# Parameter tables in a new order, late tiles and first spectral operands in steps, and the last chunk's weights loaded together: a long convolution beside a feed-forward network on one core of Trainium2

## The chip, the core and the metric

The kernel runs on one core of a Trainium2 chip. The metric is the device time of one execution in microseconds, as the median of several runs. The kernel before was run three times: 1127.53, 1129.48 and 1130.53 us, so its median is 1129.48 us. One further execution was recorded by the hardware profiler.

## The reference, cut to what matters

The input `u` has 2048 positions of 576 features. It is normalized over its features, and two branches start from the result: a state-space layer, whose convolution kernel is built from complex parameter tables of 576 x 128, and a feed-forward network. Input and both branches are added.

```python
xn = layernorm(u)                                # u: 1 x 2048 x 576
dt = exp(log_dt)[:, None]
A, Bc, Cc = A_re + 1j*A_im, B_re + 1j*B_im, C_re + 1j*C_im       # 576 x 128
P  = exp((dt*A)[:, :, None] * arange(2048))
K  = einsum("dn,dnl,dn->dl", Cc, P, dt*Bc).real  # 576 x 2048
y  = causal_convolution(xn, K) + xn * Dskip      # by FFT of length 4096
ff = silu(xn @ w1) @ w2                          # 576 -> 4608 -> 576
out = u + y + ff
```

All is in float32.

## The kernel before, in words

**Precision.** A product of two float32 matrices is made of three matmuls: each operand is split into a high part (a cast by ScalarE, ACT in the profile) and a low part (a subtraction by VectorE, DVE), and high x high, high x low and low x high are added up in PSUM. So each operand that comes from memory needs one ACT and one DVE instruction ahead of its first matmul.

**The feed-forward network is the frame.** `ffn` runs over two halves of 1024 positions, in each over nine chunks of 512 hidden features (`NCH` = 9), and in each chunk over two blocks of 512 positions. A chunk has four tiles of weights (`FT` = 4). `up(blk, t)` makes one tile of hidden values: 14 matmuls of 128x512 into `ph` (L291 to L293), then SiLU (L299), the high part `gh` (L300, ACT) and the low part `gl` (L301, DVE). `down(blk, jj)` takes 128 positions back to 576 features: 2 x 12 matmuls of 128x288 into `po` (L316), each dozen of which DVE adds to `acc` (L320). `ph` has two buffers in PSUM, `po` three. The weights of the next chunk are loaded and split between these steps: `load_w1` (L247 to L249, two tiles at once, one buffer `w1r`), `split_w1` (L260 on ACT, L262 on DVE), `load_w2` (L269, two buffers `w2r`) and `split_w2` (L278, L280). A table `after` (around L371) says after which step which of these stands; the same table held for all chunks.

**The other work is woven in.** `weave` runs through the 288 steps of the network and lets a generator, `side` (from L786), issue its next piece when a fraction of the steps has gone by; the fractions are written by hand. `side` issues in this order:

- `phase0` for the first eight tiles of 128 positions, in pairs: load (L164), layernorm (`normed`, with statistics at L180 and the normalization at L189), transposes, and stores of the normalized tile (`dxn`, L231) and of its transposes (`dxt`, L230).
- `natural` (L396 to L517), which makes the tables of the convolution kernel from the parameters, in four steps: loads (L407, L420), powers by ACT's functions, a root with its corrections (L450 to L459, the store `dexp` at L460), products, three reciprocals (L475), a second part and the store `dmag` (L517). Between them stands `phase0` for the eight later tiles, in four pairs (8, 10, 12, 14), each with load and normalization in one step, at 0.02, 0.035, 0.06 and 0.08. Their input buffer `xj` has one copy.
- `kgen` (L519 to L663), which generates the kernel and stores it as `d1k` (L659, L662), from 0.13 to 0.595 (`marks`), and between its pieces `spread`, which writes the transformed input `d1u` to memory.
- `spectral` (L665 to L706), 32 steps from 0.595 to 0.822: `front(k)` loads a tile of `d1u` and of `d1k` and splits it (`load_split`, L743 to L746, with `split_of`, L737 to L741), multiplies by the transform's matrices (`mm3`, L754, into `pu`, `pk` and `pb`) and stores the result `d`.
- `tail` (from L710): the last stage of the convolution, woven into the last chunk. `conv_load` (L761) loads `ys` from `d`, four tiles ahead, L716 loads the first half's results `r`, `add_conv` (L774 on TensorE, L780 on DVE) adds them, and L171 stores the output.

**Who sets the order.** The order in which a program issues its pieces fixes priorities; a scheduler then sorts the instructions of each engine by them, and `behind(...)` keeps an instruction from being sorted ahead of a named one. Each engine runs its own list strictly in order. Nearly all loads and many stores are issued by SyncE (SP), whose list is one queue: an issue that waits for a free buffer holds up all behind it.

Of the kernel before, what the change touches and what calls it, by code (L numbers as in the profile page):

```python
# [2 lines left out]

# [7 lines left out]
F32 = mybir.dt.float32  # L11
# [6 lines left out]
P = 128  # L18
# [23 lines left out]
def kernel(  # L42
# [91 lines left out]
    def behind(ins):  # L134
        return tc.issue_after(ins) if ins is not None else nullcontext()
# [61 lines left out]

    def phase0(p0, js):
        j0 = js[0]
        if j0 < 8:  # L200
            xs = load_x(j0, accp, "acc", (nc.sync, nc.scalar) if j0 < 4 else (nc.sync,))
            acc.update(zip(js, xs))
        else:
            xs = load_x(j0, p0, "xj", (nc.sync,))
        if j0:
            normed(p0, js, xs)
        else:
            for j, xj in zip(js, xs):
                normed(p0, (j,), (xj,))
# [23 lines left out]
    def ffn():  # L233
# [6 lines left out]
        def load_w1(half, c, t):  # L240

            f = c * FT + t
            first = half == 0 and c == 0
            r1 = (pa if first and t else wp).tile([P, 5, 2 * P], F32, tag="w1r", name="w1r", bufs=1)
            fs = slice(f * P, (f + 2) * P)
            eng = nc.gpsimd if first and t == 0 else nc.sync
            eng.dma_start(r1[:, 0:4, :], w1[0:512, fs].rearrange("(k p) f -> p k f", p=P))  # L247
            eng.dma_start(r1[0:64, 4, :], w1[512:576, fs])
            pins["load"] = eng.dma_start(r1[64:128, 4, :], w1[512:576, fs]).ins  # L249
            R1[half, c, t] = r1  # L250
# [14 lines left out]
        def load_w2(half, c, t):  # L265

            first = half == 0 and c == 0
            r2 = (pa if first and t > 1 else wp).tile([P, D], F32, tag="w2r", name="w2r", bufs=2)
            pins["load"] = nc.sync.dma_start(r2, w2v[:, c * FT + t, :]).ins  # L269
            R2[half, c, t] = r2  # L270

# [91 lines left out]
        for i, blk in enumerate(blocks):  # L363
            half, c, b = blk
            later = i + 1 < len(blocks)
            new = (half, c + 1) if c + 1 < NCH else (half + 1, 0)
            more = new[0] < 2
            if half == 0 and c == NCH - 1:
                next_xt(b)

            after = {  # L371
                (0, "u0"): [(load_w1, 0)],
                (0, "u1"): [(split_w1, 0), (load_w2, 0), (load_w2, 1)],
                (0, "u2"): [(load_w1, 2)],
                (1, "u0"): [(split_w1, 2), (split_w2, 0), (load_w2, 2)],
                (1, "d3"): [(split_w2, 1), (load_w2, 3), (split_w2, 2)],
                (1, "u2"): [(split_w2, 3)],
            }
            for step in ("u0", "d0", "d1", "d2", "d3", "u1", "u2", "u3"):
                k = int(step[1])  # L380
                if step[0] == "d":
                    down(blk, k)
                    yield 3.0
                elif later:
                    up(blocks[i + 1], k)
                    yield 3.0
                for f, t in after.get((b, step), ()) if more else ():
                    f(*new, t)
                if half == 0 and c == NCH - 1:
                    for kt in {"d3": (0, 1), "u1": (2, 3), "u2": (4,)}.get(step, ()):  # L390
                        split_xt(b, kt)
# [4 lines left out]
    def natural(nat):  # L396
# [55 lines left out]
        nc.scalar.activation(r, r, AF.Square)  # L452
        for i in range(0, 4 * D, D):

            c = slice(i, i + D)
            e = nat.tile([P, D], F32, tag="lrT", name="e")
            v.scalar_tensor_tensor(e, ex[:, c], 1.0, r[:, c], op0=ALU.subtract, op1=ALU.mult)
            v.scalar_tensor_tensor(r[:, c], e, 2.0, r[:, c], op0=ALU.add, op1=ALU.mult)
            v.scalar_tensor_tensor(ex[:, c], ex[:, c], 1.0, r[:, c], op0=ALU.add, op1=ALU.mult)  # L459
# [18 lines left out]

        v.tensor_mul(t1, t0, t0)
        v.tensor_scalar(t1, t1, 1.0, None, op0=ALU.add)  # L480
        yield

        with behind(pins["gh"]):
# [179 lines left out]
                            dskip.unsqueeze(0).broadcast_to([32, D]), accum_op=ALU.add)  # L663

    def spectral():  # L665
        def front(k):
            if k % 2 == 0:
                mm = kl.tile([P, 2, 4, P], F32R, tag="mm", name="mm")
                nc.gpsimd.dma_start(mm, cm23[:, k:k + 2])
                mats.append(mm)  # L670
            mk = mats[-1][:, k % 2]
            us, ks = load_split(d1u[k * P:(k + 1) * P, :], "u"), load_split(d1k[k * P:(k + 1) * P, :], "k")
            ka = kl.tile([P, D], F32, tag="ka", name="ka")
            kb = kl.tile([P, D], F32, tag="kb", name="kb", bufs=1)
            y = kl.tile([P, D], F32, tag="y", name="y", bufs=1)
# [65 lines left out]
        nc.vector.tensor_sub(l, t, h)  # L741
        return h, l

    def load_split(rows, tag):
        t = kl.tile([P, D], F32, tag=tag + "r", name=tag + "r")
        nc.sync.dma_start(t, rows)  # L746
        return split_of(t, tag)

    def mm3(dst, terms, hs):

# [34 lines left out]

    def side():  # L786
        nonlocal s4, kl, yp, pa, tail_at
        marks = (0.13, 0.595, 0.822)
        tail_at = (0.895, 0.0045, 0.922, 0.005)
        with tc.tile_pool(name="pa", bufs=4) as pa:  # L790
            for js in ((0, 1), (2, 3), (4, 5), (6, 7)):
# [6 lines left out]
        with tc.tile_pool(name="kf", bufs=1) as kfp:  # L798
            for n in ("f", "phi"):
                kf[n] = kfp.tile([P, D], F32, name=n + "T")  # L800
            with tc.tile_pool(name="nat", bufs=1) as nat, tc.tile_pool(name="pb", bufs=1) as pb:
                nt = natural(nat)
                tiles = iter(range(8, NJ, 2))
                for at, tables in ((0.0, 1), (0.02, 0), (0.035, 0), (gate_of(1), 1), (0.06, 0), (gate_of(2), 1), (0.08, 0), (0.085, 1)):
                    yield at
                    if tables:
                        next(nt, None)
                    else:
                        j = next(tiles)
                        with behind(pins["gl"]):  # L810
                            phase0(pb, (j, j + 1))
            with behind(pins["sd"]):
                nc.gpsimd.dma_start(f1, cf1)
            nc.sync.dma_start(vt, cv)
            with tc.tile_pool(name="up", bufs=1) as up:
                sp = spread(up)
                for n, at in enumerate(kgen()):
                    if n > 1:
                        next(sp, None)
                    yield marks[0] + at * (marks[1] - marks[0])  # L820
                for _ in sp:
                    pass
# [98 lines left out]
```

## Time and profile before

| what | value |
|---|---|
| median of the runs | 1129.48 us (1127.53 to 1130.53) |
| profiled execution | 1131.96 us |
| its span | 1130.2 us |
| mean granted clock of TensorE | 0.996 |
| chain that ended last | PE 86%, DVE 5%, DMA 5% |
| HBM read, written | 102.53 MB, 44.61 MB |

The profile shows each engine's busy time, its waits by line with what ended them, windows with the busy time, clock and DMA share, a timeline, and the chain of work that ended last, which is followed back from the last instruction. PE is TensorE's matmuls, PEld its loading of weights, SP the engine that issues DMAs. A row such as `PE po L316 <- DVE acc L320` reads: TensorE, about to write `po` in line 316, sat idle until VectorE's line 320 on `acc` was done. In slices of 28 us, the engine TensorE is at nine tenths or more but for the first ones, one in between and the last:

```profile
PE   6999899999999999999999999999999999999998
DVE  6698899999999999999999936887778778774433
DMA  9346531334242625254743345554445455336971
```

### The profile page before, as it was taken

How to read it: one execution, taken by the hardware profiler on the slowest of the kernel's cores; microseconds unless marked ns; L12 is line 12 of the kernel's file. 1: busy time of each engine (PE TensorE's matmuls, PEld its weight loads, DVE VectorE, ACT ScalarE, POOL GpSimd, SP SyncE). 2: the span in 40 equal slices, each digit the busy share in tenths (PEclk: the TensorE clock that was granted, in tenths of full speed). 3: DMA queues.
4: the chain of work that ended last, by engine and by line, in shares of the span. 5: the costliest groups of instructions: out<-in, count | busy, mean ns of one | idle time of the engine just before them, and what ended most of it. 6: DMA issues, size and time to landing. Idle time of an engine off the chain costs nothing.

```text
span 1130.2 us, 22881 instructions
## 1 busy us (share of the span) xinstructions
PE 1106.7 (98%) x9144; PEld 998.7 (88%) x9144; DVE 917.1 (81%) x1545; ACT 708.7 (63%) x1229; POOL 78.5 (7%) x130
## 2 busy tenths in 40 slices
PE   6999899999999999999999999999999999999998
PEld 5988799898888989999889998999999999998776
DVE  6698899999999999999999936887778778774433
ACT  4665356767677676676766727787777787772211
POOL 1110100000000000010000000000000000000110
PEclk9999899999999999999999999999999999999999
DMA  9346531334242625254743345554445455336971
GB/s 272 116 121 173 150 86 57 82 107 106 93 105 70 145 65 116 83 124 153 205 152 88 88 86 170 168 164 130 144 142 168 128 169 149 110 104 168 251 189 56
DMA packets 174971, 148.56 MB, mean 131 GB/s; under 512 B 110944, under 2 KB 141680, under 8 KB 174736
## 3 DMA queue, kind: packets, MB, share of 16 engines
q1 hardware_dynamic: 164768, 112.07, 37.6%
q0 software_dynamic: 9712, 34.14, 9.4%
q8 instruction: 72, 1.18, 0.4%
q10 hardware_dynamic: 384, 0.89, 0.3%
q14 instruction: 35, 0.29, 0.1%
HBM read 102.53 MB, written 44.61 MB: 130 GB/s over the span
## 4 chain that ended last, share of the span: by engine, by line
PE 86%; DVE 5%; DMA 5%; SPq 1%; issue 1%; ACT 0%; POOL 0%; DVEq 0%; POOLq 0%; ACTq 0%
PE po L316 36%; PE ph L291 30%; PE kp L631 3%; PE ph L292 3%; PE ph L293 2%; PE pk L754 2%; PE pu L754 2%; PE pb L754 2%; DMA w1r<-in_B_w_dram 2%; PE z L646 2%; PE pu L153 1%; DMA xj<-in_A_u_dram 1%; PE py L774 1%; PE pu L154 1%; DMA d1k<-stage 1%
## 5 line engine op out<-in xcount | busy, mean ns | idle before, releaser
L316 PE MATMUL po<-w2h,gh 128*128 128x288 f32 x1152 | 338.8, 297 | 6.4 <-DVE acc L320 5.7
L316 PE MATMUL po<-w2h,gl 128*128 128x288 f32 x1152 | 338.5, 297 | 1.0 <-DVE gl L301 1.0
L316 PE MATMUL po<-w2l,gh 128*128 128x288 f32 x1152 | 339.4, 296 | 0.0
L316 PEld LDWEIGHTS po<-w2h,gh 128*128 128x128 f32 x1152 | 216.1, 188 | 16.5 <-DVE acc L320 7.0
L316 PEld LDWEIGHTS po<-w2l,gh 128*128 128x128 f32 x1152 | 216.8, 188 | 4.3
L316 PEld LDWEIGHTS po<-w2h,gl 128*128 128x128 f32 x1152 | 216.5, 189 | 3.5 <-DVE gl L301 1.5
L299 ACT ACTIVATE gf<-ph 128x512 f32<-128x512 f32 (+1 forms) x148 | 86.5, 584 | 140.1 <-PE ph L293 124.7
L320 DVE TENSOR_TENSOR acc<-po,acc 128x288 f32<-128x288 f32 x288 | 126.3, 451 | 47.9 <-PE po L316 46.3
L291 PE MATMUL ph<-xh,w1h 128*128 128x512 f32 (+1 forms) x592 | 163.3, 391 | 0.5 <-ACT xh L123 0.5
L291 PE MATMUL ph<-xl,w1h 128*128 128x512 f32 (+1 forms) x592 | 161.5, 388 | 0.0
L291 PE MATMUL ph<-xh,w1l 128*128 128x512 f32 (+1 forms) x592 | 160.1, 386 | 0.0
L301 DVE TENSOR_TENSOR gl<-gf,gh 128x512 fp32r<-128x512 f32 (+1 forms) x148 | 98.7, 670 | 41.3 <-ACT gh L300 40.6
L291 PEld LDWEIGHTS ph<-xh,w1l 128*128 128x128 f32 x592 | 108.5, 189 | 20.1
L291 PEld LDWEIGHTS ph<-xl,w1h 128*128 128x128 f32 x592 | 108.5, 190 | 19.7
L291 PEld LDWEIGHTS ph<-xh,w1h 128*128 128x128 f32 x592 | 106.0, 191 | 20.0 <-issue 3.3
L300 ACT CAST gh<-gf 128x512 fp32r<-128x512 f32 (+1 forms) x148 | 89.5, 609 | 13.4 <-PE po L316 10.5
L278 ACT CAST w2h<-w2r 128x576 fp32r<-128x576 f32 x72 | 46.9, 672 | 30.6 <-PE po L316 19.5
L588 ACT ACTIVATE c<-th,magic 128x1040 f32<-128x1040 f32 x36 | 42.0, 1166 | 33.7 <-DVE C L611 25.7
L262 DVE TENSOR_TENSOR w1l<-w1r,w1h 128x640 fp32r<-128x640 f32 x72 | 56.9, 819 | 4.4 <-ACT w1h L260 4.3
L280 DVE TENSOR_TENSOR w2l<-w2r,w2h 128x576 fp32r<-128x576 f32 x72 | 53.4, 750 | 7.4 <-ACT w2h L278 7.2
L590 ACT ACTIVATE c<-th 128x1040 f32<-128x1040 f32 x36 | 38.7, 1076 | 32.6 <-DVE th L589 32.6
L292 PE MATMUL ph<-x,w1h 128*128 128x512 f32 (+1 forms) x148 | 57.2, 386 | 0.0
(182 smaller groups left out, 1836.9 us busy)
## 6 DMA issues: line engine op xcount, KB each, us to landing
w2r<-in_B_w_dram SPq DMA_DIRECT2D x72, 288.0 KB, 3.4
w1r<-in_B_w_dram SPq DMA_DIRECT2D x35, 512.0 KB, 3.9
d1u<-u POOLq DMA_DIRECT2D x32, 288.0 KB, 2.5
d1k<-stage SPq DMA_DIRECT2D x18, 512.0 KB, 7.7
ur<-d1u SPq DMA_DIRECT2D x32, 288.0 KB, 3.9
kr<-d1k SPq DMA_DIRECT2D x32, 288.0 KB, 2.8
d<-yo POOLq DMA_DIRECT2D x32, 288.0 KB, 3.9
ys<-d SPq DMA_DIRECT2D x32, 288.0 KB, 10.5
```

Of the source, the lines that this page charges most:

```text
L262: pins["w1l"] = nc.vector.tensor_sub(l1, src, h1).ins
L278: pins["w2h"] = nc.scalar.copy(h2, r2).ins
L280: nc.vector.tensor_sub(l2, r2, h2)
L291: nc.tensor.matmul(ph, w[:, kt, :], v[:, kt, a:e], start=n + kt == 0, stop=False)
L292: nc.tensor.matmul(ph, h1[:, 4, :], x4[:, a:e], start=False, stop=False)
L299: nc.scalar.activation(gf, ph, AF.Silu)
L300: pins["gh"] = nc.scalar.copy(gh, gf).ins
L301: pins["gl"] = nc.vector.tensor_sub(gl, gf, gh).ins
L316: pins["pe"] = nc.tensor.matmul(po[:, :HD], G[blk, t][g][:, js], W2[half, c, t][w][:, hs], start=n == 0, stop=n == 3 * FT - 1).ins
L320: nc.vector.tensor_add(acc[j][:, hs], po[:, :HD], acc[j][:, hs])
L588: nc.scalar.activation(c65, th, AF.Identity, bias=magic)
L754: nc.tensor.matmul(dst, st, mv[:, hs], start=n == 0, stop=n == 3 * len(terms) - 1)
```

## The change

There are four parts.

1. **Parameter tables.** `natural` has five steps in place of four. The products of the parameters, with what follows up to `t1`, move ahead of the root and its corrections, and a `yield` stands between them.
2. **Late tiles.** The load of a late pair and its normalization are two steps. The schedule of tables and tiles between 0.0 and 0.09 is a new list.
3. **First spectral operands.** `spectral` loads the operands of its first step, yields, splits them, yields, and then goes on. `load_split` becomes `load_part`, which only loads. Two of the marks move by 0.002 and 0.001.
4. **The last chunk's weights.** For the last chunk of the second half the table `after` is another: both pairs of w1 and all four tiles of w2 are loaded after the first step of the block ahead, and half of these buffers (`w1r` for the second pair, `w2r` for the tiles 2 and 3) come from the pool `yp` of the tail, which opens when the spectral part's pool has closed.

The core of the diff:

```diff
-        if j0 < 8:
-            xs = load_x(j0, accp, "acc", (nc.sync, nc.scalar) if j0 < 4 else (nc.sync,))
-            acc.update(zip(js, xs))
-        else:
-            xs = load_x(j0, p0, "xj", (nc.sync,))
+        xs = load_x(j0, accp, "acc", (nc.sync, nc.scalar) if j0 < 4 else (nc.sync,))
+        acc.update(zip(js, xs))
...
+            last = half == 1 and c == NCH - 1
-            r1 = (pa if first and t else wp).tile([P, 5, 2 * P], F32, tag="w1r", name="w1r", bufs=1)
+            r1 = (pa if first and t else yp if last and t else wp).tile([P, 5, 2 * P], F32, tag="w1r", name="w1r", bufs=1)
...
-            r2 = (pa if first and t > 1 else wp).tile([P, D], F32, tag="w2r", name="w2r", bufs=2)
+            r2 = (pa if first and t > 1 else yp if last and t > 1 else wp).tile([P, D], F32, tag="w2r", name="w2r", bufs=2)
...
+            if new == (1, NCH - 1):
+
+                after = {
+                    (0, "u0"): [(load_w1, 0), (load_w2, 0), (load_w2, 1), (load_w1, 2), (load_w2, 2), (load_w2, 3)],
+                    (0, "u1"): [(split_w1, 0)],
+                    (1, "u0"): [(split_w1, 2), (split_w2, 0)],
+                    (1, "d3"): [(split_w2, 1), (split_w2, 2)],
+                    (1, "u2"): [(split_w2, 3)],
+                }
...
         yield
-
-        with behind(pins["gh"]):
-            nc.scalar.activation(r, ex, AF.Abs_reciprocal_sqrt, bias=neg1)
...
-        nc.sync.dma_start(dexp, ex[:, :3 * D].rearrange("n (d k) -> n d k", k=3))
         pr, pi, t0, t1 = tl("pr"), tl("pi"), tl("t0"), tl("t1")
...
         v.tensor_scalar(t1, t1, 1.0, None, op0=ALU.add)
+        yield
+
+        with behind(pins["gh"]):
+            nc.scalar.activation(r, ex, AF.Abs_reciprocal_sqrt, bias=neg1)
...
+        nc.sync.dma_start(dexp, ex[:, :3 * D].rearrange("n (d k) -> n d k", k=3))
         yield
...
+        def operands(k):
+            rows = slice(k * P, (k + 1) * P)
+            return load_part(d1u[rows, :], "u"), load_part(d1k[rows, :], "k")
...
-            us, ks = load_split(d1u[k * P:(k + 1) * P, :], "u"), load_split(d1k[k * P:(k + 1) * P, :], "k")
+            us, ks = ops.pop(k) if k in ops else (split_of(t, n) for t, n in zip(operands(k), "uk"))
...
+        first = operands(0)
+        yield 1.1
+        with behind(pins["gh"]):
+            ops = {0: [split_of(t, n) for t, n in zip(first, "uk")]}
+        yield 1.12
         nxt = front(0)
...
-        marks = (0.13, 0.595, 0.822)
+        marks = (0.13, 0.597, 0.823)
...
-                tiles = iter(range(8, NJ, 2))
-                for at, tables in ((0.0, 1), (0.02, 0), (0.035, 0), (gate_of(1), 1), (0.06, 0), (gate_of(2), 1), (0.08, 0), (0.085, 1)):
+                def late(j):
+
+                    xs = load_x(j, pb, "xj", (nc.sync,))
+                    yield
+                    with behind(pins["gl"]):
+                        normed(pb, (j, j + 1), xs)
+                    yield
+
+                tiles = chain.from_iterable(late(j) for j in range(8, NJ, 2))
+                for at, todo in ((0.0, nt), (0.0, tiles), (0.004, tiles), (0.005, tiles), (gate_of(0), nt), (0.026, tiles), (0.028, tiles), (0.036, tiles), (0.038, tiles), (gate_of(1), nt), (0.06, tiles), (gate_of(2), nt), (0.09, nt)):
                     yield at
-                    if tables:
-                        next(nt, None)
-                    else:
-                        j = next(tiles)
-                        with behind(pins["gl"]):
-                            phase0(pb, (j, j + 1))
+                    with behind(pins["gl"] if at else None):
+                        next(todo, None)
```

`gate_of(i)` is (4 + 8i + 1)/288, that is 0.017, 0.045 and 0.073 for 0, 1 and 2.

More of the change, by code (lines that the diff above doesn't have):

```diff
@@ L1 @@
 import math
+from itertools import chain
 from contextlib import ExitStack, nullcontext
@@ L267, in load_w2 @@
             first = half == 0 and c == 0
-            r2 = (pa if first and t > 1 else wp).tile([P, D], F32, tag="w2r", name="w2r", bufs=2)
+            last = half == 1 and c == NCH - 1
+            r2 = (pa if first and t > 1 else yp if last and t > 1 else wp).tile([P, D], F32, tag="w2r", name="w2r", bufs=2)
             pins["load"] = nc.sync.dma_start(r2, w2v[:, c * FT + t, :]).ins
```

18 lines of the change are left out of this document (9 added, 9 removed).

## The prediction

> **What bounds the kernel now.** I read the page first, then TensorE's waits over the whole span, then the windows in which TensorE is not full, then the timeline and the chain of waits around each gap.
>
> ```profile
> span 1130.2 us, 22881 instructions
> PE 1106.7 (98%) x9144; PEld 998.7 (88%) x9144; DVE 917.1 (81%) x1545; ACT 708.7 (63%) x1229; POOL 78.5 (7%) x130
> ```
>
> TensorE is busy for 1106.7 us of 1130.2, so only 23.5 us are idle. The change adds no matmul and removes none; it can only give or take idle time, and time at a reduced clock. So the first question is what the 23.5 us consist of. Each row of TensorE's waits: line waited for, us in total, times, longest.
>
> ```profile
> PE pt L122 <- DVE xn L189: 9.0, 1, 9.0
> PE po L316 <- DVE acc L320: 5.7, 2, 3.7
> PE pk L754 <- ACT kh L740: 1.3, 1, 1.3
> PE po L316 <- DVE gl L301: 1.0, 2, 0.7
> PE pt L126 <- DVE xl L124: 0.9, 1, 0.9
> PE po L316 <- ACT w2h L278: 0.7, 1, 0.7
> ```
>
> The 9.0 and the 0.9 are the start, before the first layernorm is there, and the change does not touch it, nor what follows the last matmul. Within its reach are 5.7 (3.7 and 2.0), 1.3, one 0.7 behind gl and one 0.7 behind w2h. Where they lie, and what the clock does there, the windows tell (columns: stretch, its length, busy us and count of PE, PEld, DVE, ACT, POOL, granted clock, DMA share, GB/s).
>
> ```profile
> 100.00:120.00 20.00, 20.00 (x123) 18.08 (x121) 19.68 (x34) 5.85 (x9) 1.74 (x1) 1.00 0.57 142
> 125.06:131.89 6.83, 6.16 (x24) 5.89 (x24) 6.74 (x15) 4.04 (x7) 3.24 (x1) 0.50 0.42 173
> 140.00:640.00 500.00, 500.00 (x5102) 451.16 (x5101) 477.93 (x719) 341.95 (x515) 20.99 (x38) 1.00 0.41 108
> 1028.00:1032.00 4.00, 4.00 (x32) 4.00 (x31) 1.08 (x3) 0.00 (x0) 0.00 (x0) 1.00 0.52 128
> 1032.00:1056.00 24.00, 24.00 (x177) 18.19 (x175) 7.78 (x15) 6.62 (x11) 1.97 (x4) 1.00 1.07 264
> 1056.00:1060.00 4.00, 2.02 (x16) 1.78 (x15) 3.73 (x8) 1.44 (x3) 0.00 (x0) 1.00 0.42 84
> 1060.00:1088.00 28.00, 28.00 (x225) 20.89 (x224) 12.04 (x25) 6.69 (x11) 5.80 (x12) 1.00 1.06 261
> ```
>
> There are four places. Between 20 and 140 us VectorE is nearly full, and something stalls after 120, where the clock falls. From 140 to 640 TensorE is never idle. One gap stands near 687, where the spectral part begins, and one at 1056, in the last steps. In 125.06 to 131.89 the clock was 0.50.
>
> **The change part by part.** First 20 to 140 us, with the timeline there (start, duration, instruction, idle ahead and its releaser).
>
> ```profile
> 120.78 1.54 DVE L180 BATCH_NORM_STATS2 st<-xj 128x6 f32<-128x288 f32 x4 [1.10 <-DMA xj<-in_A_u_dram]
> 122.24 1.15 DVE L516 TENSOR_TENSOR wt<-wt,ex 128x576 f32<-128x576 f32 x1
> 123.30 0.45 DVE L320 TENSOR_TENSOR acc<-po,acc 128x288 f32<-128x288 f32 x1
> ...
> 123.81 0.40 PE L316 MATMUL po<-w2h,gh 128*128 128x288 f32 x1 [3.67 <-DVE acc L320]
> ```
>
> VectorE reaches the statistics of the last late pair of tiles before its load has landed, waits 1.10 us, then does 1.54 us of statistics and 1.15 us of a table, and only then adds up the FFN's result, for which TensorE has waited 3.67 us. Right after it the clock falls to 0.50 for 6.83 us, of which 6.16 are busy: at half speed half of that, 3.1 us, is lost. The old step issues load and normalization together; the new one issues the load a step earlier. In the built order the load of each of the last two pairs precedes its statistics by a whole step. So these stalls go: 0.7 + 3.7 + 0.7 + 3.1 = **8.2 us removed**.
>
> A rule of the Trainium skill is to be weighed here. Its page "TensorE: Matmul & The Clock Gate", section "What's actually happening", says that the clock falls to a half after an idle window of about 3.4 us, and that the window runs freely. The trace agrees as far as it goes: an idle of 3.7 us was followed by 0.50, idles of 2.0 and 1.3 were not. By this rule, what I remove is worth more than its idle time, and any new gap over the same bound costs more than its length; the sum below would not change.
>
> What becomes late next in this stretch? The tiles are moved ahead of other work, and SP's queue is in order. The rows of the DMA issues (between 20 and 140 us: count, KB each, median us to landing) and of VectorE's groups and waits there:
>
> ```profile
> dxn<-xj SPq DMA_DIRECT2D x4, 576.0 KB, 4.3
> xj<-in_A_u_dram SPq DMA_DIRECT2D x15, 144.0 KB, 3.3
> ```
>
> ```profile
> L180 DVE BATCH_NORM_STATS2 st<-xj 128x6 f32<-128x288 f32 x16 | 6.1, 445 | 4.6 <-DMA xj<-in_A_u_dram 4.6
> L475 DVE RECIPROCAL t<-t 96x256 f32<-96x256 f32 x3 | 5.0, 1701 | 0.0
> ```
>
> ```profile
> DVE st L180 <- DMA xj<-in_A_u_dram: 4.6, 3, 2.2
> ```
>
> The tile xj has one buffer. In the new order the load of pair 10 stands on SP behind six table loads, eight stores of transposes and the store dxn of pair 8, which must land first (4.3), then the load itself (3.3). Its statistics stand on VectorE ahead of a split of w1, for which the next `up` waits, and the next w1 load waits in turn for that split. VectorE waited for xj three times before, 4.6 us in all, 1.5 each. I expect two such waits to stay (pair 10, and pair 14, whose load also follows its predecessor's store). VectorE is 19.68 of 20 busy, so a wait of it passes through: 2 x 1.5 = 3.0. The other new orders (three reciprocals of 1.7 behind one another; ACT's root ahead of w1's casts) have the same instructions as before, where 100 to 120 holds no idle of TensorE, and the buffers of PSUM cover one accumulation of 1.6 (12 matmuls of 0.133, worked out further on); I add 0.2. **New: 3.2**, bounds 0 (loads early enough) and 7.4 (two times the 3.7 of the row above).
>
> From 140 to 640 VectorE has 477.93 of 500 and TensorE is full; the kernel generation has the same instructions and nearly the same marks. Cost 0; if VectorE's margin of 4% were used up, a few tenths.
>
> **Spectral start.** The chain of waits between 667 and 687:
>
> ```profile
> 667.00 8.51 DMA d1k<-stage
> ...
> 680.14 6.47 DMA kr<-d1k
> ```
>
> Store, an addition of the skip term and load follow one another, and TensorE waits 1.3 for the split. In the new order the operands are loaded at the mark, split at 1.1 and multiplied at 1.12 of a scale on which the 32 pairs follow, some steps later, so the chain has over ten us more. **1.3 removed**; bound below 0, if the store of d1k is what is late.
>
> **The last steps.** On the chain the two pieces that matter, and rows of SP and TensorE:
>
> ```profile
> 1024.58 0.52 PE pb L754 x4
> ...
> 1027.02 7.96 PE po L316 x60
> ...
> 1043.59 11.82 DMA w1r<-in_B_w_dram
> ```
>
> ```profile
> 1071.33 2.72 PE ph L291 x12
> ```
>
> ```profile
> 1028.50 1.28 SPq L761 DMA_DIRECT2D ys<-d  x2
> ...
> 1043.59 0.60 SPq L249 DMA_DIRECT2D w1r<-in_B_w_dram  x1
> 1045.26 4.63 SPq L761 DMA_DIRECT2D ys<-d  x4
> 1058.89 0.35 SPq L269 DMA_DIRECT2D w2r<-in_B_w_dram  x1
> ```
>
> The second pair of the last chunk's w1 is issued at 1043.59 behind ten ys loads and three of r, lands at 1055.4, and its two splits come ahead of the accumulation that TensorE waits for: the 2.0 of the waits. SP itself then stands until 1058.89 at a w2 load whose buffer is not free, and DMA falls to 0.42 in 1056 to 1060. After the change all these weights are issued in one step: w1's second pair follows four ys loads, and two w2 loads in buffers of their own follow it. **2.0 removed.**
>
> What is given back here? In the built order 338 `po` and 148 `ph` matmuls stand behind the last spectral one (`pb`), where 359 and 154 stood. By the rows 7.96/60 = 0.133 and 2.72/12 = 0.227 that is 21 x 0.133 + 6 x 0.227 = 4.2 us less work in which the ys stream, which starts only when the last d is stored, can run. The tile to watch is the eleventh (22 of 32 ys loads), which TensorE takes between the last `up` steps:
>
> ```profile
> 1078.49 0.69 PE L774 MATMUL py<-ys,s 64*32 64x288 f32 x8
> ```
>
> From 1024.6 to 1078.5 are 53.9, less the stall of 2.0 is 51.9, less 4.2 is 47.7 us after the last pb. By then must land: 22 ys of 288 KB, 4 r of 576, w1's pair of 640, two w2 of 288 and about eight output stores of 144 (sizes by the shapes in the code, four bytes an element), that is 11,008 KB or 11.3 MB; at 262 GB/s (264 and 261 in the two windows) 43.0 us. The stream begins 3.9 after the pb (1028.50), and its first 4 us run at 128, which loses 2.0: 48.9 us. Lateness 1.2 by bytes alone; the last ys of a tile lands some 2 us behind the mean of the stream when it shares the engines with stores, so up to 3.2. I take the upper end, as earlier conv tiles can wait some tenths too: **3.2 new**, bounds 0 and 6 (a rate lower by a tenth would add 4.8 to the 1.2).
>
> **Sum.** 8.2 - 3.2 + 1.3 + 2.0 - 3.2 = 5.1 us faster. The profiled execution took 1131.96 us (span 1130.2), so 1126.9; it lies 2.5 above the median of the runs, 1129.48, and the same sum taken from that gives **1124.4**.
>
> **Rivals.** About 0.3%, 3.4 us, is what a measurement of this kernel can tell from no change.
>
> (A) All old stalls go and nothing new comes: 8.2 + 1.3 + 2.0 = 11.5, 1118. For it: loads get a whole step of lead. Against: one xj buffer, and 47.7 us for 48.9 us of stream. Chance 0.20.
>
> (B) The ys stream comes late in one piece. At the upper bound of 6 the gap passes the 3.7 after which the clock fell, and 3.1 more is lost: 9.1 in place of 3.2, sum -0.8, about **1130**. The Trainium skill's page "TensorE: Matmul & The Clock Gate", section "What's actually happening", with its idle window of about 3.4 us, is the rule that would make it so. For it: 4.2 us less room and more loads in front. Against: the stalls may be split over several tiles, each under 2. Chance 0.24.
>
> (C) Slower: pair 10's statistics block VectorE for the whole of the store and the load behind it. Store and load follow one another on one buffer, 4.3 + 3.3 = 7.6, and both can share the engines with table loads. If VectorE arrives as the store is issued, it waits 7.6, TensorE follows with that less what PSUM covers (one accumulation, 1.6 by 12 x 0.133), 6.0, and the clock falls, 3.1; the same for pair 14: 18.2 in place of 3.2, sum -9.9, 1139; for one pair 9.1 + 1.5, sum -2.3, 1132. It decides when the wait on VectorE exceeds 5.3 (1.6 + 3.7). For it: SP's order. Against: the longest such wait before was 2.2. Chance 0.14 for one or both.
>
> That the change doesn't do what it says, the loads being issued no earlier because the buffer isn't free, is the same as (C) in its mild form, the forecast's 2 x 1.5.
>
> **How the numbers follow.** The forecast has 0.42, with 1121.5 to 1127.5 as its own range (new stalls 0.3 to 6.3 instead of 6.4 at the fast end, and up to 3 more at the slow one). Faster than 1126.1 are (A) 0.20 and some 0.36 of the forecast: 0.56. Within 1126.1 to 1132.9: the forecast's 0.06, 0.20 of (B) and 0.04 of (C): 0.30. Slower: 0.04 of (B), 0.10 of (C): 0.14. The range leaves out half of (A) and most of the slower share: 1118.5 to 1132.
>
> **What would show it.** Right: no row `po <- DVE acc` of 3.7 near 120 and a clock of 1.00 up to 140; VectorE's wait for xj below 4.6 in total, with two waits near 60 and 115; no `pk <- ACT kh`; no w1r on the chain at 1043; TensorE idle behind ys or acc in the last 70 us, about 3 us, in its place. Wrong: a clock of 0.50 anywhere, TensorE idle between 140 and 640, or a wait of VectorE for xj over 5.

## The result and the profile after

The changed kernel took 1133.71 us (median of 6 runs, 1132.41 to 1134.37), the kernel before 1129.53 us (6 runs, the three from above among them). The ratio is 1.0037, with a 95% interval of 1.0026 to 1.0049: slower by 0.37%, where 0.45% faster was forecast. The profiled execution of the changed kernel took 1134.37 us, that of before 1131.96.

The first lines of the profile, and TensorE's waits over the whole span (line waited for, us in total, times, longest):

```profile
span 1132.6 us, 22870 instructions
## 1 busy us (share of the span) xinstructions
PE 1108.6 (98%) x9144; PEld 998.8 (88%) x9144; DVE 916.8 (81%) x1545; ACT 709.3 (63%) x1229; POOL 73.0 (6%) x130
```

```profile
PE pt L123 <- DVE xn L190: 8.9, 1, 8.9
PE py L793 <- DMA ys<-d: 5.8, 4, 2.1
PE po L316 <- DVE gl L301: 1.8, 2, 1.5
PE po L316 <- ACT w2h L278: 0.9, 2, 0.6
PE ph L291 <- ACT xh L124: 0.7, 1, 0.7
PE ph L291 <- ACT w1h L259: 0.6, 1, 0.6
PE ph L291 <- DVE w1l L261: 0.3, 1, 0.3
```

The 5.7 behind `acc` and the 1.3 behind `kh` are gone, as forecast. In their place stands a wait that the kernel before did not have at all: 5.8 us for the `ys` loads of the last convolution stage. The windows of the changed kernel say where idle time and reduced clock lie (columns as above):

```profile
100.00:120.00 20.00, 20.00 (x125) 18.23 (x124) 17.67 (x33) 5.29 (x8) 1.07 (x1) 1.00 0.51 122
120.00:140.00 20.00, 18.43 (x104) 16.13 (x103) 14.48 (x24) 7.38 (x12) 2.01 (x2) 0.91 0.59 169
140.00:640.00 500.00, 498.87 (x5093) 449.16 (x5092) 480.46 (x722) 343.41 (x517) 22.08 (x40) 1.00 0.40 107
...
680.00:700.00 20.00, 20.00 (x128) 18.62 (x127) 14.10 (x26) 15.13 (x31) 0.00 (x0) 1.00 0.38 115
...
1020.00:1040.00 20.00, 19.00 (x136) 16.68 (x134) 7.62 (x15) 5.06 (x9) 0.54 (x1) 1.00 0.55 144
1040.00:1060.00 20.00, 16.69 (x117) 12.93 (x118) 7.75 (x15) 4.26 (x7) 3.91 (x8) 0.91 1.08 252
1060.00:1080.00 20.00, 19.38 (x145) 15.37 (x144) 7.96 (x16) 4.84 (x8) 1.93 (x4) 1.00 1.07 261
1080.00:1100.00 20.00, 19.16 (x178) 14.77 (x179) 8.15 (x18) 1.85 (x4) 2.90 (x6) 1.00 0.73 176
```

From 1020 to 1100 TensorE is idle for 5.77 us (1.00 + 3.31 + 0.62 + 0.84), where the kernel before had 1.98. The clock of 1040 to 1060 was 0.91: from 1056.43 on, 3.4 us ran at half clock. Three of the four gaps stand at the second, third and fourth tile of the convolution that TensorE takes; the fourth, at 1080.85, is shown further on:

```profile
1039.97 0.69 PE L793 MATMUL py<-ys,s 64*32 64x288 f32 x8 [0.99 <-DMA ys<-d]
1048.90 0.84 PE L793 MATMUL py<-ys,s 64*32 64x288 f32 x16 [1.23 <-DMA ys<-d]
1055.18 0.84 PE L793 MATMUL py<-ys,s 64*32 64x288 f32 x16 [2.08 <-DMA ys<-d]
```

The last spectral matmul divides the loss from the gain. Its row in the kernel before, then in the changed one:

```profile
1024.81 0.29 PE L754 MATMUL pb<-yh,mm 128*128 128x288 f32 x1
```

```profile
1025.73 0.29 PE L773 MATMUL pb<-yh,mm 128*128 128x288 f32 x1
```

It comes 0.9 us later, but with 4.2 us more of the network's matmuls ahead of it (21 x 0.133 + 6 x 0.227, as in the prediction): up to there the change gained 3.3 us. From its end to the end of the span are 105.1 us before and 106.6 after, with 4.2 us less work: 5.7 us lost. Together that is the 2.4 us by which the spans differ.

### The profile page after: what moved, and what is told of

It reads as the page before. It is cut to its first block, busy times and chain, and to the rows that moved or that the text cites. A ratio compares the mean times of both kernels' runs of the same rounds, so it can differ in the third digit from the quotient of the medians.

```text
span 1132.6 us, 22870 instructions
## 1 busy us (share of the span) xinstructions
PE 1108.6 (98%) x9144; PEld 998.8 (88%) x9144; DVE 916.8 (81%) x1545; ACT 709.3 (63%) x1229; POOL 73.0 (6%) x130
## 4 chain that ended last, share of the span: by engine, by line
PE 77%; DMA 7%; DVE 7%; issue 4%; SPq 2%; ACT 2%; POOL 0%; ACTq 0%; DVEq 0%; POOLq 0%
PE po L316 33%; PE ph L291 27%; DMA ys<-d 3%; PE kp L641 3%; PE ph L293 2%; PE ph L292 2%; PE pu L773 2%; PE pk L773 2%; PE pb L773 2%; PE z L656 2%; PE pu L154 1%; SPq L228 1%; DVE st L181 1%; DMA xj<-in_A_u_dram 1%; DVE gl L301 1%
## 5 line engine op out<-in xcount | busy, mean ns | idle before, releaser
L291 PE MATMUL ph<-xh,w1l 128*128 128x512 f32 (+1 forms) x592 | 162.5, 387 | 0.3 <-DVE w1l L261 0.3
L293 PE MATMUL ph<-x,w1l 128*128 128x512 f32 (+1 forms) x148 | 57.1, 386 | 0.0
```

What stands on the lines that cost most here:

```text
L291: nc.tensor.matmul(ph, w[:, kt, :], v[:, kt, a:e], start=n + kt == 0, stop=False)
L293: pins["pe"] = nc.tensor.matmul(ph, l1[:, 4, :], x4[:, a:e], start=False, stop=True).ins
```

## The experiments

Theory after the result: the change gains where it was meant to, in the first 140 us and at the start of the spectral part, and loses more at the end, because the built order leaves less work of TensorE behind the last spectral matmul, and the `ys` stream, which can only start there, comes too late. Rivals: the new weight loads of the last chunk, which stand ahead of most `ys` loads, cost the time; or the new order of tables and tiles does. The waits for `ys` in the table are those of the one profiled execution of each run, and that can lie far from the median: e4's took 1132.21 us, e5's 1125.58.

| run | po, ph behind the last spectral matmul | wait for ys, us | median, us | ratio to before (95%) |
|---|---|---|---|---|
| changed kernel | 338, 148 | 5.8 | 1133.71 | 1.0037 (1.0026 to 1.0049) |
| e1 changed, old marks | 359, 154 | 0 | 1126.08 | 0.9978 (0.9962 to 0.9994) |
| e2 changed, old last weights | 338, 148 | 1.2 | 1133.94 | 1.0044 (1.0028 to 1.0060) |
| e3 before, new tables and tiles | 390, 208 | 0 | 1125.78 | 0.9966 (0.9950 to 0.9983) |
| e4 before, new last weights | 359, 154 | 1.9 | 1129.26 | 1.0001 (0.9987 to 1.0016) |
| e5 changed, last mark 0.836 | 359, 154 | 0.3 | 1127.77 | 0.9996 (0.9978 to 1.0014) |
| e6 changed, old marks and old weights | 359, 154 | 0 | 1128.29 | 0.9999 (0.9987 to 1.0012) |
| e7 changed, marks 0.595, 0.815 | 377, 154 | 0 | 1125.39 | 0.9969 (0.9957 to 0.9981) |
| e8 changed, marks 0.590, 0.800 | 384, 185 | 0 | 1125.38 | 0.9974 (0.9963 to 0.9985) |
| e9 changed, marks 0.610, 0.840 | 288, 144 | 8.7 | 1139.27 | 1.0082 (1.0056 to 1.0108) |
| e10 before, new marks | 376, 177 | 0 | 1129.90 | 1.0005 (0.9991 to 1.0019) |
| e11 changed, old weights, 0.595, 0.815 | 377, 154 | 0 | 1125.26 | 0.9957 (0.9941 to 0.9973) |

**e1: the old marks in the changed kernel.**

```diff
-        marks = (0.13, 0.597, 0.823)
+        marks = (0.13, 0.595, 0.822)
```

> The changed kernel with the two old marks (0.595, 0.822). In the built order 359 po and 154 ph matmuls then stand behind the last spectral matmul, as in the kernel before, where the changed kernel has 338 and 148: 4.2 us more work of TensorE in which the ys stream can run. Theory (the changed kernel loses its gain because the ys stream starts too late for the work that is left): TensorE's wait for ys falls from 5.8 us to about 1.6, the clock stays at 1.00 between 1040 and 1060, and the time is about 5 us below the changed kernel, near 1128.5. Rival (the loss comes from the new order of tables and tiles between 20 and 140 us): the wait for ys may shrink, but the time stays within 2 us of the changed kernel, near 1133.

Measured 1126.08 us, 7.6 below the changed kernel. Its windows at the end show no idle time and a full clock:

```profile
1040.00:1060.00 20.00, 20.00 (x164) 17.03 (x163) 8.82 (x18) 4.59 (x8) 3.92 (x8) 1.00 1.07 269
1060.00:1080.00 20.00, 20.00 (x145) 14.12 (x144) 8.75 (x17) 6.38 (x11) 3.88 (x8) 1.00 1.08 258
```

The theory's direction holds; the wait fell to 0, further than the expected 1.6, and the time further than the expected 1128.5. Two numbers in `marks`, changed by 0.002 and 0.001, carry the whole loss of the median. Ten of the 12 executions took 1125.1 to 1127.8 us; the other two took 1132.05 and 1133.19, with a mean clock of 0.995, so with this order the last stage seems to be in time by a narrow margin only.

**e2: the normal weight loads for the last chunk in the changed kernel.**

```diff
-            if new == (1, NCH - 1):
+            if False:
...
-            r1 = (pa if first and t else yp if last and t else wp).tile([P, 5, 2 * P], F32, tag="w1r", name="w1r", bufs=1)
+            r1 = (pa if first and t else wp).tile([P, 5, 2 * P], F32, tag="w1r", name="w1r", bufs=1)
...
-            r2 = (pa if first and t > 1 else yp if last and t > 1 else wp).tile([P, D], F32, tag="w2r", name="w2r", bufs=2)
+            r2 = (pa if first and t > 1 else wp).tile([P, D], F32, tag="w2r", name="w2r", bufs=2)
```

> The changed kernel with the normal table of weight loads for the last chunk (its fourth part undone). The work behind the last spectral matmul stays at 338 and 148. Theory (stream too late): w1's second pair and two w2 tiles, 1.2 MB or 4.7 us at 262 GB/s, no longer stand ahead of most ys loads, so the wait for ys falls from 5.8 to about 1 to 2, but the wait for acc behind the late w1 pair, 2.0 in the kernel before, comes back at 2 to 4: in all 1 to 3 us faster than the changed kernel, 1131 to 1133. Rival (the last weights were not what was late): within 1 us of the changed kernel.

Measured 1133.94 us: no gain, the expectation of 1 to 3 us was wrong. The waits of its TensorE:

```profile
PE po L316 <- DVE acc L320: 5.7, 1, 5.7
...
PE py L793 <- DMA ys<-d: 1.2, 1, 1.2
```

The wait for `ys` falls to 1.2 as expected, but the wait behind the late second pair of w1 comes back at 5.7 and not at 2 to 4. With as little room as here the time is the same with either order of the weight loads; the order decides which wait carries the lateness.

**e3: the new tables and tiles alone.** The kernel before with `phase0`, `natural` and the list of the changed kernel, nothing else; of the list:

```diff
-                tiles = iter(range(8, NJ, 2))
-                for at, tables in ((0.0, 1), (0.02, 0), (0.035, 0), (gate_of(1), 1), (0.06, 0), (gate_of(2), 1), (0.08, 0), (0.085, 1)):
+                tiles = chain.from_iterable(late(j) for j in range(8, NJ, 2))
+                for at, todo in ((0.0, nt), (0.0, tiles), (0.004, tiles), (0.005, tiles), (gate_of(0), nt), (0.026, tiles), (0.028, tiles), (0.036, tiles), (0.038, tiles), (gate_of(1), nt), (0.06, tiles), (gate_of(2), nt), (0.09, nt)):
```

> The kernel before with the first two parts alone (tables in five steps, late tiles in two steps each, new list). In its built order the last spectral matmul stands earlier, with 390 po and 208 ph behind it, so the ys stream cannot be late. Theory: the stretch from 20 to 140 us gains about 3 us over the profiled execution of before (idle 5.4 and a clock of 0.83 in one slice there, against 2.6 and 0.91 in the changed kernel), so the kernel is faster than before by 1 to 3 us. Rival (the new order of this stretch costs): slower than before by 1 to 3 us, with TensorE's idle between 60 and 650 above that of before.

Measured 1125.78 us, 3.1 below before: the theory's upper end. TensorE's waits from 60 to 140 us hold 1.4 behind `gl`, 0.6 and 0.2, and 1020 to 1100 is full. Since its last spectral matmul also stands earlier, part of the 3.1 is the stall of 2.0 at the end; what the tables and tiles gain without it is bounded by e10 and e11.

**e4: the new last weights alone.** The kernel before with the special table `after` and the `yp` buffers; of the table:

```diff
+            if new == (1, NCH - 1):
+
+                after = {
+                    (0, "u0"): [(load_w1, 0), (load_w2, 0), (load_w2, 1), (load_w1, 2), (load_w2, 2), (load_w2, 3)],
...
```

> The kernel before with the fourth part alone (the last chunk's weights loaded together, half of them in the tail's pool). 359 and 154 behind the last spectral matmul, as before. Theory: the wait of 2.0 for acc behind w1 goes, and the ys stream with 1.2 MB ahead of it comes 1 to 2 us late in its place: within 1 us of before, 1128.5 to 1130.5. Rival (the loads at the front cost as much as the whole loss of the changed kernel): 3 to 5 us slower than before.

Measured 1129.26 us, ratio 1.0001: as the theory had it. The stall of 2.0 is gone and one of 1.9 for `ys` stands in its place. What the clock did after that is worth seeing; windows of e4 there:

```profile
1072.00:1076.00 4.00, 2.14 (x16) 1.12 (x14) 0.20 (x1) 1.21 (x2) 0.00 (x0) 1.00 1.06 291
1076.00:1080.00 4.00, 4.00 (x15) 2.07 (x16) 1.51 (x3) 0.00 (x0) 1.17 (x3) 0.53 1.08 247
1080.00:1084.00 4.00, 4.00 (x26) 2.43 (x25) 0.00 (x0) 0.62 (x2) 0.76 (x2) 0.62 1.09 274
```

An idle of 1.9 us was followed by 6.8 us at half clock. This execution was one of the slower ones of e4 (1132.21 us, where the 12 executions lie between 1126.57 and 1133.00).

**e5: the last mark moved further back.**

```diff
-        marks = (0.13, 0.597, 0.823)
+        marks = (0.13, 0.597, 0.836)
```

> The changed kernel with the spectral part's last mark moved further back, from 0.823 to 0.836. By its mark the ys stream starts later; in the built order, however, 359 po and 154 ph matmuls stand behind the last spectral matmul (338 and 148 in the changed kernel), and SP's list from the first ys load on is the same. Theory (what counts is the work of TensorE that stands behind the last spectral matmul): 4.2 us more room, wait for ys from 5.8 to under 2, time near that of the run with the old marks, 1126 to 1127. Rival (what counts is the mark, that is the share of steps at which the spectral part is asked for): as late as the changed kernel or later, 1134 and above.

Measured 1127.77 us, 5.9 below the changed kernel, with 0.3 us of wait for `ys`. The median lies 0.8 above the expected band; the rival, 1134 and above, is out. So what the mark asks for is not what decides: a later mark gave an earlier last spectral matmul in the scheduler's order, and the time followed the order. The 12 executions spread from 1125.38 to 1135.70 us, so the median alone makes e5 look better against the kernel before than it is: the ratio, 0.9996, says no difference from it.

**e6: old marks and old weight loads in the changed kernel.** The edit of e2 and that of e1:

```diff
-            if new == (1, NCH - 1):
+            if False:
...
-        marks = (0.13, 0.597, 0.823)
+        marks = (0.13, 0.595, 0.822)
```

> The changed kernel with the old marks and the normal table of weight loads for the last chunk, so that only the tables, the late tiles and the first spectral operands are new. 359 and 154 behind the last spectral matmul. Theory: the ys stream is in time, and what stays is the wait for acc behind the late second pair of w1, about 2.0 as in the kernel before: 1.5 to 2.5 us slower than the run with the old marks and the new weight loads, 1127.5 to 1128.5. Rival (with the stream in time the weight loads cost nothing either way, since their wait only changes its name): within 0.7 us of 1126.1.

Measured 1128.29 us, 2.2 above e1, with this wait, where e1 has none:

```profile
PE po L316 <- DVE acc L320: 1.4, 1, 1.4
```

As expected in time, with a gap of 1.4 and not 2.0.

**e7 and e8: an earlier spectral part** in the changed kernel; e7, and for e8 (0.13, 0.590, 0.800):

```diff
-        marks = (0.13, 0.597, 0.823)
+        marks = (0.13, 0.595, 0.815)
```

> The changed kernel with marks 0.595 and 0.815. 377 and 154 behind the last spectral matmul, 2.4 us more work than with the old marks. Theory: no wait for ys is left to take, so the time stays at 1126.1, within 1 us, and is that of the best version. Rival (an earlier end of the spectral part crowds the steps before it, where VectorE and the queue of loads have less room): 1 to 3 us slower than 1126.1, with idle of TensorE between 690 and 1020.

> The changed kernel with marks 0.590 and 0.800. 384 and 185 behind the last spectral matmul, 10.3 us more work than with the old marks. Theory: as the run with 0.595 and 0.815, 1126.1 within 1 us, no wait for ys; the kernel generation, which ends at 0.590, is squeezed a little, a few tenths of idle between 140 and 640. Rival (crowding): 2 to 5 us slower, with a wait for kr or d1k at the start of the spectral part.

Measured 1125.39 and 1125.38 us, no wait of TensorE from 640 us to the end in either. More room lowers the median by only 0.7 us against e1, and the steps before are not crowded. It does take away the slow executions: of the 36 executions of e1, e5 and e6, with 359 and 154, eight took over 1131 us; of the 31 of e3, e7, e8 and e11, with more behind the last spectral matmul, none took over 1127.82.

**e9: a later spectral part** in the changed kernel.

```diff
-        marks = (0.13, 0.597, 0.823)
+        marks = (0.13, 0.610, 0.840)
```

> The changed kernel with marks 0.610 and 0.840: 288 po and 144 ph stand behind the last spectral matmul, 50 and 4 less than in the changed kernel, so 7.5 us less room for the ys stream; SP's list from the first ys load on is the same. Theory (room behind the last spectral matmul sets the wait for ys, one for one): 7 to 8 us slower than the changed kernel, 1140 to 1142, with 12 to 14 us of wait for ys and a clock under 1.00 behind the longer ones. Rival (the stream is late only by a fixed amount, once it is late): near 1134.

Measured 1139.27 us, 5.6 above the changed kernel for 7.5 us less room; the wait for `ys` is 8.7, not 12 to 14. The rival of a fixed lateness is out, but one for one is not right either. Its largest gap:

```profile
1081.89 1.18 PE L793 MATMUL py<-ys,s 64*32 64x288 f32 x8 [5.81 <-DMA ys<-d]
```

It is the same tile that the prediction watched. Counted by the place of the last spectral matmul, as for the changed kernel above, the last stage alone is not far from the theory: from the end of that matmul to the end of the span it loses 6.9 us more than the changed kernel's. Up to there this execution is 3.1 us better, of which 1.7 is a loss of clock near 125 us that it does not have.

**e10: the new marks in the kernel before.**

```diff
-        marks = (0.13, 0.595, 0.822)
+        marks = (0.13, 0.597, 0.823)
```

> The kernel before with the two new marks alone. In its built order 376 po and 177 ph then stand behind the last spectral matmul (359 and 154 before), 7.5 us more. Theory: the marks themselves cost nothing here; the stall of 2.0 in the last steps goes, as the second pair of w1 is issued earlier with the stream, and the stalls of 20 to 140 and of 687 stay: 1126.5 to 1128.5, with a clock that drops near 125 in some executions. Rival (later marks cost, whatever the order): 1132 and above.

Measured 1129.90 us, ratio 1.0005: above the expected 1126.5 to 1128.5. The stall at the end is gone, and so is the one at 687, but TensorE is now idle for 1.82 us between 140 and 640, where the kernel before was full. That leaves some 1.5 us of the expected gain for which the trace shows no reason. The rival, 1132 and above, is out. The window:

```profile
140.00:640.00 500.00, 498.18 (x5093) 449.57 (x5093) 479.82 (x720) 344.15 (x516) 21.52 (x39) 1.00 0.42 108
```

**e11: old weight loads with the earlier spectral part.** The edits of e2 and of e7 in the changed kernel:

```diff
-            if new == (1, NCH - 1):
+            if False:
...
-        marks = (0.13, 0.597, 0.823)
+        marks = (0.13, 0.595, 0.815)
```

> The changed kernel without its fourth part and with marks 0.595 and 0.815, so that 377 and 154 stand behind the last spectral matmul. Theory: w1's second pair is issued 2.4 us earlier against TensorE's work than with the old marks, where it cost a wait of 1.4, so no wait is left in the last 120 us, and the time is that of the same marks with the new weight loads, 1125.4 within 0.7. Rival (the new weight loads have a gain of their own): 1.5 to 3 us slower, with a wait for acc or w2.

Measured 1125.26 us, the lowest time of all and within 0.2 of e7. Its windows at the end:

```profile
1040.00:1060.00 20.00, 20.00 (x173) 16.98 (x179) 9.45 (x19) 5.62 (x9) 3.16 (x7) 1.00 0.93 268
1060.00:1080.00 20.00, 20.00 (x152) 14.20 (x144) 8.08 (x18) 5.45 (x9) 3.86 (x8) 1.00 1.08 246
```

So the fourth part has no gain of its own once the spectral part ends early enough. And e10 and e11 both have no idle of TensorE from 1020 to 1100: between them the tables, the tiles, the first operands and other marks, which no run here separates, are worth 1129.90 - 1125.26 = 4.6 us.

## Why the prediction was wrong

**The step that failed is the last term of the sum**, the new wait for `ys`, which I took as 3.2 with bounds 0 and 6. It measured 5.8 us of idle in four pieces and 3.4 us at half clock, which cost some 1.7 more: 7.5. The mechanism was right, a stream with less room than it needs, and the room was right: 47.7 us forecast; 47.4 in the trace, without its waits and the loss at half clock. The need was too small. By the forecast the 22nd `ys` load lands 48.9 to 50.9 us after the last spectral matmul; it was used at

```profile
1080.85 0.69 PE L793 MATMUL py<-ys,s 64*32 64x288 f32 x8 [1.46 <-DMA ys<-d]
```

which is 54.8 after that matmul's end at 1026.0 (the forecast counted from half a us earlier, where its group begins). The prediction also gave the earlier tiles "some tenths" of wait; they waited 4.3 of the 5.8 us. Their loads stand right behind the new weights, which is the likely reason; with the old weight loads (e2) the waits for `ys` are 1.2 in all. The window from the first `ys` issue to that moment shows why, with SP's rows of the stream:

```profile
1029.41:1080.71 51.30, 45.67 (x325) 35.83 (x323) 20.01 (x39) 13.43 (x22) 5.84 (x12) 0.97 1.04 248
```

```profile
1029.41 1.28 SPq L780 DMA_DIRECT2D ys<-d  x2
...
1032.66 0.61 SPq L246 DMA_DIRECT2D w1r<-in_B_w_dram  x1
...
1047.25 14.12 SPq L780 DMA_DIRECT2D ys<-d  x8
...
1063.07 21.04 SPq L780 DMA_DIRECT2D ys<-d  x14
```

51.3 us at 248 GB/s are 12.7 MB, where I had counted 11.3. In that window 12 output stores of 144 KB were issued, not 8, which is 0.6 MB more. And 29 `ys` loads were issued, not 22: most of the other 0.8 MB must be parts of loads behind the one that matters, which were moved before it landed. I had counted only what stands ahead in the queue, at a rate of 262.

Two things in the code bear on this, and I had both wrong. `conv_load` runs six tiles ahead (`AHEAD` = 6 in both kernels), not four as written above. And the tile that I called the eleventh is the eleventh in the order of the loads, but the eighth that TensorE takes: by the marks in `tail_at` the loads for the tiles 8, 9 and 10 (counted from 0) are asked for before those of tile 7, and TensorE takes these three only from 1085.70 us on. Six loads, 1.8 MB or by my estimate 7 us at 248 GB/s, stand ahead of the one that is waited for without being needed first. Another order of these loads was not tried.

**The 3.1 us of half clock were counted as if every execution had them in full.** Of 74 further executions of the kernel before, 34 had a mean clock of 0.998 and a median of 1128.0 us, 7 had 0.995 and 1132.2. The profiled one, 1131.96 at 0.996, lies towards the upper end, and I took the sum from it to the median unchanged. Some loss of clock is in each of them, though: none of the 74 has a mean clock of 0.999 or more, which 29 of the 31 executions of e3, e7, e8 and e11 have. So there is such a gain, but it seems to be smaller than 3.1 in most executions. Of the 4.2 us between the medians, 2.4 are the difference of the profiled spans; the other 1.8 is that the profiled execution of before lay 2.4 above its median, and that of the changed kernel 0.7.

**20 to 140 us: near in idle time, wrong in the clock and in detail.** Before, then after:

```profile
20.00:140.00 120.00, 114.56 (x705) 104.56 (x704) 101.21 (x196) 63.92 (x101) 14.88 (x9) 0.97 0.55 151
20.00:140.00 120.00, 117.09 (x717) 105.42 (x716) 100.94 (x195) 64.07 (x102) 8.78 (x8) 0.99 0.57 154
```

Idle went from 5.4 to 2.9 us. That is a gain of 2.5, where stalls of 5.1 less 3.2 of new ones gave 1.9. That 2.9 is near the forecast 3.2 is luck, as the new stalls come from elsewhere. VectorE's wait for `xj` did not fall, it rose, and the remaining gap has another releaser than I named:

```profile
DVE st L181 <- DMA xj<-in_A_u_dram: 6.6, 3, 2.4
```

```profile
122.04 0.87 ACT L195 ACTIVATE xj<-xj,mb,sd 128x576 f32<-128x576 f32 x1
...
122.81 0.60 ACT L300 CAST gh<-gf 128x512 fp32r<-128x512 f32 x1
...
123.21 0.68 DVE L301 TENSOR_TENSOR gl<-gf,gh 128x512 fp32r<-128x512 f32 x1
...
123.94 0.53 PE L316 MATMUL po<-w2h,gl 128*128 128x288 f32 x2 [1.46 <-DVE gl L301]
```

ACT does part of a late tile's normalization ahead of the cast of `gh`, VectorE makes `gl` after it, and TensorE waits 1.46. Behind this gap the clock fell as well, for 3.4 us where the kernel before had 6.8, so of the 3.1 us of clock only some 1.4 were gained in this execution:

```profile
124.00:126.00 2.00, 2.00 (x7) 1.68 (x8) 2.00 (x3) 1.97 (x5) 0.00 (x0) 0.65 0.60 242
126.00:128.00 2.00, 2.00 (x7) 1.61 (x7) 2.00 (x5) 0.39 (x1) 0.00 (x0) 0.50 0.44 68
```

**140 to 640: wrong by 1.1.** I gave it nothing; TensorE was idle for 1.13 us: 0.6 behind ACT's split of a w2 tile, 0.3 behind VectorE's of a w1 pair and 0.2 behind ACT's `stage`. What made these late was not tested.

**The spectral start: right.** 1.3 us gone, 680 to 700 is full.

**The stall of 2.0 behind w1: right that it goes,** and e2 and e4 show that it is tied to the stream: with little room the lateness only changes its name. But it is not the same thing in every order: in e6, where the stream is in time, the old weight loads still cost a wait of 1.4, which e1 lacks.

**The sum with what was measured.** 2.5 + 1.4 for the first stretch, less 1.1, plus 1.3, plus 2.0, less 7.5, plus 0.6 by which the start was shorter, is 0.8 us slower; the profiled spans say 2.4. The other 1.6 us are not accounted for.

**The rivals.** (A) did not come, as the first stretch kept a gap and the last got one. (B), the late stream, is the nearest, with 0.24. Its condition did not hold: the longest gap was 2.1 us and not over 3.7, and the clock fell all the same. That its price of 9.1 is not far from 7.5 is luck in part. I let it end at no change, since I set it against a gain that held 3.1 us of clock. (C), a blocked VectorE, did not come: its longest wait for `xj` was 2.4, under the 5.3 from which it would decide. The chance of 0.56 for faster rested on the term that I had least ground for, a stream with 47.7 us of room and 48.9 of need by my own count. Two of the signs of being wrong that the prediction names came: a clock of 0.50, and idle of TensorE between 140 and 640.

**Room and need.** Room and time are not one for one: 4.2 us of room were worth 5.9 to 7.6 us (e5, e1), 7.5 us more only 5.6 (e9). The traces show part of the reason. Call room the time from the end of the last spectral matmul to the tile that the prediction watched, without waits and without half of the time at half clock, and need the time from the same matmul to the landing of that tile's second load, the 22nd:

| run | room, us | need, us | need less room, us |
|---|---|---|---|
| changed kernel | 47.4 | 54.7 | 7.3 |
| e1 | 51.1 | 49.6 | -1.5 |
| e5 | 51.2 | 51.4 | 0.2 |
| e4 | 51.2 | 52.9 | 1.7 |
| e9 | 39.1 | 51.3 | 12.2 |

The loss up to this tile is what the need has over the room, in each of these single executions. The need is no constant: e9 has 8.3 us less room than the changed kernel, but needs 3.4 us less.

**What stays open.** Why the need lies at 49.6 in one trace and at 54.7 in another is not worked out; the loads and stores that run beside the stream are the likely reason, and e1, e5 and e4 differ in it by 3.3 us with the same count behind the last spectral matmul. And idle and clock up to that matmul would make a gain of some 5 us (3.4 of idle, about 1.5 of clock), where 3.3 were counted by its place.

## What to carry to other kernels

Where a stream of loads can only start when a stage has ended, compare its need with the work that is left behind that stage in the built order, and count in the need also the loads that are issued behind the critical one and the stores beside them. Ask too whether all the loads ahead of the critical one are needed before it. A mark in a schedule is only a request: read where the last instruction of the stage stands in the order, since a later mark can give an earlier place. And before a clock drop is put into a sum, ask how large it is in the other executions, by their mean clocks.

## What the runs showed of the hardware

The clock of TensorE fell to a half after gaps far shorter than the 3.7 us of the kernel before: after 1.46 us near 124 and 2.08 near 1055 in the changed kernel, and after 1.9 in e4. Yet in e1, e2 and e3 a gap at the same place near 124 of 1.2 to 1.4 was followed by a clock of 1.00, in e6, e7 and e8 one of 1.46 or 1.47, and in the kernel before one of 1.98 near 1057.

The clock records of the traces say more. The stretches between two changes of the clock last whole multiples of 3.413 us: half clock 3.41 or 6.83; full clock for example 105.81 (31 times), 71.68 (21 times) and 928.42 (272 times) in the changed kernel. So the clock changes on a fixed grid of 3.41 us. Cut along this grid, the gap of 1.98 of the kernel before falls into two steps, and the gap of 2.08 of the changed kernel into one; two rows of each:

```profile
1053.49:1056.90 3.41, 2.78 (x31) 1.92 (x29) 0.63 (x1) 1.39 (x3) 0.00 (x0) 1.00 1.09 218
1056.90:1060.32 3.42, 2.07 (x15) 2.07 (x16) 3.42 (x9) 0.54 (x1) 0.07 (x1) 1.00 0.25 48
```

```profile
1053.02:1056.43 3.41, 1.33 (x20) 0.81 (x20) 3.41 (x7) 0.00 (x0) 0.00 (x0) 1.00 1.06 301
1056.43:1059.84 3.41, 3.41 (x17) 3.41 (x16) 0.94 (x3) 0.00 (x0) 1.93 (x4) 0.50 1.10 207
```

In the 13 traces, between the first full clock and 1100 us, 11 steps of full clock hold 1.57 us or more of idle time of TensorE, and nine of them are followed by half clock: all seven with 1.86 or more, and two of the four below. None with 1.52 or less is. So where a gap falls on the grid decides as much as its length. Between 1.57 and 1.77 both outcomes occur, and why is open.

The Trainium skill's page "TensorE: Matmul & The Clock Gate", section "What's actually happening", gives an idle window of about 3.4 us that runs freely. The traces agree with the length of the window and with its running freely: the drops near 124 us start at 122.72, 123.88, 124.59 and 125.06 in four traces, at four places of the grid against the start of the kernel. They do not agree that the window has to be idle throughout: 1.57 us of idle in 3.41 were enough here.

So a small gap can cost more than its length. e6, with one gap of 1.4 us in the last stage, has a median 2.9 above e7, which has none. Of its 12 executions, the seven with a mean clock of 0.999 or more took 1126.2 to 1128.8 us, the five below it 1128.9 to 1133.0.
